# Moving one batch's tail rows to the last block of a fused linear-attention and MLP kernel

## The chip, the cores and the metric

The kernel runs on one core of one Trainium2 chip. The metric is the device time of one launch in microseconds (us). Inputs and output are float32 in device memory (HBM); all matrix products run in bf16 with float32 accumulation.

## The reference

Eight batches of eight heads, 576 positions, head size 64. Cosine-weighted linear attention is followed by a two-layer MLP with a sigmoid-approximated GELU over the 4608 rows of 512 columns:

```python
def phi(x, c, s):                       # c, s: cos and sin of pi/2 * position / 576
    r = np.maximum(x, 0.0)
    return np.concatenate([r * c, r * s], axis=-1)      # 64 -> 128 features
q_p, k_p = phi(q, cos_w, sin_w), phi(k, cos_w, sin_w)
kv  = np.einsum('bhsf,bhsd->bhfd', k_p, v)
z   = np.sum(k_p, axis=2)
x   = einsum('bhsf,bhfd->bhsd', q_p, kv) / (einsum('bhsf,bhf->bhs', q_p, z) + 1e-6)
# heads side by side: x is 4608 x 512
h   = x @ w_in                          # w_in  512 x 2048
g   = h * (1.0 / (1.0 + np.exp(-1.702 * h)))
out = g @ w_out                         # w_out 2048 x 512
```

## The kernel before, in words

**Blocks and tails.** A block is the MLP of one batch, and while TensorE runs it, the attention of the next batch is prepared. Of the 576 rows of a batch, 512 go through the block: `mm1(b, fc)` makes one of 16 slices of the hidden layer (4 matmuls of 128x512 into a PSUM tile `mm`, then ScalarE's GELU into `g`), and `mm2(b, t, lo, hi)` sums the slices `lo` to `hi` into output chunk `t` of 128 rows (one 128x512 matmul for each slice). After the last slice ScalarE copies the chunk to `ysb`, and a DMA stores it. The 64 rows left over of each batch are its tail. Tails lie side by side in `xt` (before the GELU) and `gt` (after it), 64 columns for each batch. Two neighbouring tails make one output chunk, `mm2(u, 4, ...)` for u = 1, 3, 5, 7.

**Where the tails are worked.** The tails of batches 0 and 1 are worked early by `mm1_tail_first`: 2 x 32 matmuls of 64 columns for each of these batches, at the end of that batch's first layer. Their chunk, `mm2(1, 4, 0, FC)`, stands in block 1. The other six tails are worked in the last block by `mm1_tails(fc)`: 64 matmuls of 384 columns in all.

**Preparing the next batch inside a block.** VectorE makes the weighted features of q (`trig_q`, into `qn`) and k (`trig`, into `kr`), and casts v into `vt` (`vcopy`). DMA transposes turn `qn` into `qT` (`qturn_dma`, line 196). Then TensorE makes k^T v (`kv_mm`, line 214; 72 matmuls, evacuated to `kvs` by VectorE in `kv_evac`), and for each of five chunks of 128 rows the numerators and denominators (`num_mm`, line 227; 8 matmuls). VectorE divides (`num_div`, lines 235 to 239, result `xn`), and a DMA transpose writes `xn` into the input `xT` of the next block (`xturn_dma`, line 268; chunk 4, the tail, goes to `xt`). I call these five chunks x0 to x4. The first matmul of the next block reads all 512 columns of `xT`, thus x0 to x3.

**Order.** The program text sets the order on every engine (`manual_schedule`): each engine takes its instructions as they are written, and waits only on data and buffers. In block 1 TensorE has, after its first layer: the tail of batch 1 (line 300), k^T v of batch 2, the tails' chunk (16 matmuls), and then four output chunks in halves of 8 matmuls, with x0 to x4 of batch 2 behind the first five halves. Blocks 2 to 6 do the same without the two tail steps. `pat` holds two PSUM tiles (`at`) for k^T v and the numerators, `pmm` four for all else.

**Queues.** SyncE's queue (SP) issues, in the order of the program, the transposes and, from `load_next`, the loads of q, k and v two batches ahead; POOL's queue issues the early loads and the stores of line 335. Only the very last half chunk is stored from SP.

Of the kernel before, what the change touches and what calls it, by code (L numbers as in the profile page):

```python
# [11 lines left out]
AF = mybir.ActivationFunctionType  # L12
# [7 lines left out]
def kernel(  # L20
# [9 lines left out]
    nc = tc.nc  # L30
    B, H, S, D = q.shape
    d_model = H * D
    d_ff = moe_w_in.shape[1]
    KC = d_model // 128
    FC = d_ff // 128
# [85 lines left out]
    def wcol(kc, fc):  # L121

        g, c = divmod(fc, 4)
        w = w_in_t[g][:, kc, :] if g < 2 else w_in_t[2][:, kc, ts(g - 2, 512)]
        return w.rearrange("p (f c) -> p f c", c=4)[:, :, c]
# [68 lines left out]
    def qturn_dma(c):  # L194
        n = 128 if c < 4 else 64
        nc.sync.dma_start_transpose(out=qT[:, :, c * 128:c * 128 + n],
                                    in_=qn[0:n, c].rearrange("p h f -> p (h f)"))
# [3 lines left out]
    def kv_open(i0=0, i1=NI):  # L201
        t = pat.tile([128, 2, 512], F32, name="at")
        for i in range(i0, i1):
            st["kv", i] = t[:, :, ds((i - i0) * 65, 65)]
        st["ps", i0] = t[:, :, 0:(i1 - i0) * 65]
        if i0 == 0:
            st["kvs"] = small.tile([128, 2, NI, VW], BF16, name="kvs", bufs=2)

    def kv_mm(i0, i1, rhs, col, n):
        for i in range(i0, i1):  # L210
            for j in range(NS):
                for hh in range(2):
                    r = slice(hh * 64, hh * 64 + 64)
                    nc.tensor.matmul(st["kv", i][:, hh, ds(col, n)], kr[r, j, i, :], rhs(r, i, j),  # L214
                                     start=(j == 0), stop=(j == NS - 1))

    def kv_evac(i0, i1):
        o = st["kvs"][:, :, i0:i1, 0:65]
        nc.vector.tensor_copy(o, st["ps", i0].rearrange("p hh (i e) -> p hh i e", e=65))  # L219
# [3 lines left out]
    def num_mm(c):  # L223
        ps = pat.tile([128, 2, 512], F32, name="at")
        for h in range(H):
            i, hh = divmod(h, 2)
            nc.tensor.matmul(ps[:, h // 4, ds((h % 4) * 65, 65)], qT[:, h, ts(c, 128)],  # L227
                             st["kvs"][:, hh, i, 0:65], start=True, stop=True)
        nums[c] = [ps]

    def num_div(c):
        ps = nums[c][0]
        pv = ps[:, :, 0:260].rearrange("p a (h e) -> p a h e", h=4)
        den = small.tile([128, 2, 4], F32, name="den")
        nc.vector.tensor_scalar(den, pv[:, :, :, 64], 1e-6, None, op0=ADD)  # L235
        inv = small.tile([128, 2, 4], F32, name="inv")
        nc.vector.reciprocal(inv, den)  # L237
        xn = small.tile([128, 2, 4, 64], BF16, name="xn", bufs=4)
        nc.vector.tensor_tensor(xn, pv[:, :, :, 0:64],  # L239
                                inv.unsqueeze(3).to_broadcast([128, 2, 4, 64]), op=MUL)  # L240
        nums[c].append(xn)
# [6 lines left out]
    def x_cols(b, c):  # L248
        return x[b][:, :, ts(c, 128)] if c < 4 else xt[:, :, ts(b, 64)]
# [15 lines left out]
    def xturn_dma(b, c):  # L265
        xn = nums.pop(c)[1]
        n = 128 if c < 4 else 64
        nc.sync.dma_start_transpose(out=x_cols(b, c),
                                    in_=xn[0:n].rearrange("p a h e -> p (a h e)"))
# [17 lines left out]
    def mm1(b, fc):  # L287
        mm1_part(b, fc, 0, MT)
        gelu(fc)
# [3 lines left out]
    xt = one.tile([128, KC, B * 64], BF16, name="xt")  # L293
    gt = one.tile([128, FC, B * 64], BF16, name="gt")

    def mm1_tail_first(b, half):
        hps = pmm.tile([128, 8, 64], F32, name="mm")
        for f in range(8):
            for kc in range(KC):
                nc.tensor.matmul(hps[:, f], wcol(kc, half * 8 + f), xt[:, kc, ts(b, 64)],  # L300
                                 start=(kc == 0), stop=(kc == KC - 1))
        nc.scalar.activation(gt[:, ts(half, 8), ts(b, 64)], hps, AF.Gelu_apprx_sigmoid)

    def mm1_tails(fc):
        hps = pmm.tile([128, MT], F32, name="mm")
        for kc in range(KC):
            nc.tensor.matmul(hps[:, 128:B * 64], wcol(kc, fc), xt[:, kc, 128:B * 64],  # L307
                             start=(kc == 0), stop=(kc == KC - 1))
        nc.scalar.activation(gt[:, fc, 128:B * 64], hps[:, 128:B * 64], AF.Gelu_apprx_sigmoid)

    yp = {}
    out_j = out[0:S].rearrange("(p j) d -> j p d", j=NS)
# [1 line left out]
    def rows(b, t):  # L314

        if t == 4:
            return [(64 * u, 64, out_j[NS - 1] if b + u == 1 else out[(b + u) * S - 64:(b + u) * S])
                    for u in range(2)]
        if b == 0:
            return [(64 * u, 64, out_j[2 * t + u]) for u in range(2)]  # L320
        return [(0, 128, out[b * S:b * S + 512].rearrange("(p c) d -> c p d", c=4)[t])]

    def mm2(b, t, lo, hi, c0=0, c1=d_model, last=False):
        if lo == 0:
            yp[b, t, c0] = pmm.tile([128, d_model], F32, name="mm")
        for fc in range(lo, hi):
            w = gT[fc][:, ts(t, 128)] if t < 4 else gt[:, fc, ts(b // 2, 128)]
            nc.tensor.matmul(yp[b, t, c0][:, c0:c1], w, w_out_sb[:, fc, c0:c1],  # L328
                             start=(fc == 0), stop=(fc == FC - 1))
        if hi == FC:  # L330
            ysb = ypool.tile([128, d_model], F32, name="ysb")
            nc.scalar.activation(ysb[:, c0:c1], yp[b, t, c0][:, c0:c1], AF.Identity)  # L332
            for p0, n, dst in rows(b, t):
                eng = nc.sync if last else nc.gpsimd
                eng.dma_start(out=dst[:, c0:c1], in_=ysb[p0:p0 + n, c0:c1])  # L335

    def idle(n, cols=512):
# [10 lines left out]
    def start_block(b, opened=False):  # L348

        if not opened:  # L350
            xturn_mm(0)
            xturn_evac(b, 0)
            xturn_mm(1)
            xturn_evac(b, 1)
            num_mm(2)
            num_div(2)
        for c in range(4):
            for fc in range(4):
                mm1_part(b, fc, c * 128, c * 128 + 128)
            if c == 0:  # L360
                num_mm(3)
                num_div(3)
                xturn_mm(2)
                xturn_evac(b, 2)
            if c == 1:
                num_mm(4)
                num_div(4)
                xturn_mm(3)
                xturn_evac(b, 3)
        for fc in range(4):  # L370
            gelu(fc)
        mm1(b, 4)
        xturn_mm(4)
        xturn_evac(b, 4)
# [52 lines left out]
        trig(kr, kf, j)  # L427
    for fc in range(5, FC):
        mm1(0, fc)
    mm1_tail_first(0, 0)  # L430
    mm1_tail_first(0, 1)
    for c in range(5):
        trig_q(c, act=(c > 2))
        qturn_dma(c)
# [27 lines left out]
    mm2(0, 3, 12, 16)  # L462
    start_block(1, opened=True)


    for b in range(1, B):
        nb = b + 1 if b + 1 < B else None
        f0 = 5 if b == 1 else 0
        for fc in range(f0, FC):
            if nb is not None and fc == f0:  # L470
                for c in range(5):
                    trig_q(c)
                    qturn_dma(c)
            if nb is not None and fc == f0 + 1:
                for j in range(NS):
                    trig(kr, kf, j)
                vcopy(0, 4)
                if nb + 1 < B:
                    load_next(nb + 1)
            mm1(b, fc)  # L480
        if nb is not None:
            x_open(nb)
        if b == 1:
            mm1_tail_first(1, 0)
            mm1_tail_first(1, 1)
        if nb is not None:
            kv_open()
            kv_mm(0, 4, vt_rhs, 0, 65)
            kv_evac(0, 4)
        if b == 1:  # L490
            mm2(1, 4, 0, FC)
        if nb is None:
            for fc in range(FC):
                mm1_tails(fc)
            for u in range(3, B, 2):
                mm2(u, 4, 0, FC)
        for t in range(4):
            last = nb is None and t == 3
            if last:
                mm2(b, t, 0, FC, 0, 256)  # L500
                mm2(b, t, 0, FC, 256, 512, last=True)
                continue
            mm2(b, t, 0, 8)
            if nb is not None and t < 3:
                num_mm(2 * t)
                num_div(2 * t)
                xturn_dma(nb, 2 * t)
            mm2(b, t, 8, 16)
            if nb is not None and t < 2:
                num_mm(2 * t + 1)  # L510
                num_div(2 * t + 1)
                xturn_dma(nb, 2 * t + 1)


# [28 lines left out]
```

## Time and profile before

| What | Value |
|---|---|
| Median of 3 runs (lowest, highest) | 294.02 us (294.0, 294.31) |
| The profiled execution: its own time | 294.29 us |
| Its span, first to last instruction | 292.6 us |
| TensorE busy | 284.0 us, 97% of the span |
| VectorE, ScalarE, POOL busy | 123.6, 128.7, 57.5 us |
| Mean granted TensorE clock | 0.998 |
| DMA traffic | 53.54 MB; q1 (issued by SP) 35.53 MB, q0 (by POOL) 17.63 MB |

The profile is of one execution, whose own time lies 0.27 us above the median. Times in it count from its first instruction. PE is TensorE's matrix unit, DVE is VectorE, ACT is ScalarE; SPq and POOLq are the instruction sequencers of SyncE and GpSimd. The chain of waits is the work that ended last, followed backwards from the end, and shows in what order the time was spent.

### The profile page before, as it was taken

To read this page: it belongs to the slowest core of one execution; us is meant where nothing else is said; L and a number is where in the kernel's file an instruction comes from. 1 tells how busy PE (TensorE), PEld (TensorE's weight loads), DVE (VectorE), ACT (ScalarE), POOL (GpSimd) and SP (SyncE) were. 2 spreads that over 40 slices of the span, in tenths; PEclk is the share of its full clock that TensorE was granted. 3 is DMA by queue.
4 is the path that set the end of the run, shared out by engine and by line. 5 is a ranking of instruction groups with operands and counts; after the bars stand their busy time and mean duration, and the time that the engine had idled before them with its cause. 6 is when DMAs were issued, how large, how long until landed. Compare 5 with 4: busy or idle time off the path is not lost.

```text
span 292.6 us, 6031 instructions
## 1 busy us (share of the span) xinstructions
PE 284.0 (97%) x2461; PEld 157.6 (54%) x2461; DVE 123.6 (42%) x355; ACT 128.7 (44%) x224; POOL 57.5 (20%) x70
## 2 busy tenths in 40 slices
PE   8979999999999999999999999999999999999993
PEld 3775646857545554555555554555455545564452
DVE  4774415881478047903691269225931510000000
ACT  7947733663116611562146304631464136771111
POOL 6350003200216001600061014201330110001211
PEclk9999999999999999999999999999999999999999
DMA  7999999999989964999598859895840430001311
GB/s 252 240 224 286 347 179 238 370 205 245 382 161 182 303 248 116 176 249 312 136 176 243 306 142 166 208 357 137 152 99 2 104 97 25 1 0 38 72 72 72
DMA packets 72731, 53.54 MB, mean 183 GB/s; under 512 B 52608, under 2 KB 62464, under 8 KB 72704
## 3 DMA queue, kind: packets, MB, share of 16 engines
q1 hardware_dynamic: 66160, 35.53, 49.6%
q0 software_dynamic: 6544, 17.63, 22.5%
q8 instruction: 19, 0.31, 0.4%
q14 instruction: 8, 0.07, 0.1%
HBM read 36.70 MB, written 9.44 MB: 158 GB/s over the span
## 4 chain that ended last, share of the span: by engine, by line
PE 93%; DMA 4%; DVE 1%; POOL 0%; issue 0%; ACT 0%; ACTq 0%
PE mm L328 43%; PE mm L279 38%; PE mm L307 4%; PE at L227 3%; PE at L214 3%; DMA vb<-in_v_dram 2%; PE mm L300 1%; DMA kf<-in_k_dram 1%; PE at L256 1%; DVE xn L239 1%; POOL vb L139 0%; DVE inv L237 0%; PE mm L182 0%; DVE den L235 0%; ACT ysb L332 0%
## 5 line engine op out<-in xcount | busy, mean ns | idle before, releaser
L328 PE MATMUL mm<-w_out_sb,g 128*128 128x512 bf16 (+1 forms) x528 | 117.4, 372 | 0.0
L279 PE MATMUL mm<-xT,w_in 128*128 128x512 bf16 (+1 forms) x608 | 113.5, 345 | 0.0
L284 ACT ACTIVATE g<-mm 128x512 bf16<-128x512 f32 x128 | 75.6, 598 | 32.0 <-PE mm L279 31.9
L335 POOL DMA_DIRECT2D out_dram<-ysb x44 | 46.4, 1057 | 216.8 <-ACT ysb L332 216.7
L279 PEld LDWEIGHTS <-w_in 128*128 128x128 bf16 x608 | 61.7, 113 | 49.1
L328 PEld LDWEIGHTS <-g 128*128 128x128 bf16 x528 | 48.8, 98 | 50.0
L332 ACT ACTIVATE ysb<-mm 128x512 f32<-128x512 f32 (+1 forms) x37 | 21.7, 586 | 115.8 <-PE mm L328 115.8
L219 DVE CAST kvs<-at 128x520 bf16<-128x520 f32 (+1 forms) x9 | 5.8, 642 | 56.4 <-PE at L214 56.4
L239 DVE TENSOR_TENSOR xn<-at,inv 128x512 bf16<-128x512 f32 x40 | 27.6, 691 | 1.4
L153 DVE TENSOR_SCALAR kr<-kf,cosw 128x256 bf16<-128x256 f32 x68 | 23.3, 343 | 9.1 <-DMA kf<-in_k_dram 9.1
L153 DVE TENSOR_SCALAR kr<-kf,sinw 128x256 bf16<-128x256 f32 x68 | 23.5, 346 | 0.0
L235 DVE TENSOR_SCALAR den<-at 128x8 f32<-128x8 f32 x40 | 6.6, 166 | 37.1 <-PE at L227 37.1
L227 PEld LDWEIGHTS <-qT 128*128 128x128 bf16 x320 | 14.5, 97 | 7.3
L166 DVE TENSOR_SCALAR qn<-qf,cosw 128x512 bf16<-128x512 f32 (+1 forms) x33 | 15.7, 477 | 3.8 <-DMA qf<-in_q_dram 3.8
L227 PE MATMUL at<-kvs,qT 128*128 128x65 bf16 x320 | 15.9, 193 | 0.0
L166 DVE TENSOR_SCALAR qn<-qf,sinw 128x512 bf16<-128x512 f32 (+1 forms) x33 | 15.8, 477 | 0.0
L328 PE MATMUL mm<-w_out_sb,gt 128*128 128x512 bf16 x64 | 14.2, 379 | 0.0
L214 PEld LDWEIGHTS <-kr 64*128 64x128 bf16 x648 | 10.3, 94 | 4.0 <-issue 3.1
L307 PE MATMUL mm<-xt,w_in 128*128 128x384 bf16 x64 | 10.6, 326 | 0.0
L328 PEld LDWEIGHTS <-gt 128*128 128x128 bf16 x64 | 6.2, 97 | 7.3
L174 DVE CAST vt<-vf 128x2304 bf16<-128x2304 f32 (+1 forms) x7 | 8.9, 1264 | 0.6 <-DMA vf<-in_v_dram 0.6
L307 PEld LDWEIGHTS <-w_in 128*128 128x128 bf16 x64 | 7.2, 113 | 3.3
(57 smaller groups left out, 101.5 us busy)
## 6 DMA issues: line engine op xcount, KB each, us to landing
kf<-in_k_dram SPq DMA_DIRECT2D x6, 1152.0 KB, 9.4
vf<-in_v_dram SPq DMA_DIRECT2D x6, 1152.0 KB, 12.3
out_dram<-ysb POOLq DMA_DIRECT2D x27, 256.0 KB, 2.7
qf<-in_q_dram SPq DMA_DIRECT2D x6, 1024.0 KB, 6.9
out_dram<-ysb POOLq DMA_DIRECT2D x17, 128.0 KB, 6.1
w_out_sb<-in_moe_w_out_dram POOLq DMA_DIRECT2D x4, 512.0 KB, 18.1
kf<-in_k_dram POOLq DMA_DIRECT2D x1, 1152.0 KB, 12.3
vf<-in_v_dram POOLq DMA_DIRECT2D x1, 1152.0 KB, 20.6
```

The costliest lines, as they stand in the source:

```text
L153: nc.vector.tensor_scalar(o, i, 0.0, w[:, j:j + 1], op0=MAX, op1=MUL)
L166: nc.vector.tensor_scalar(o, i, 0.0, sc, op0=MAX, op1=MUL)
L174: nc.vector.tensor_copy(o, i)
L214: nc.tensor.matmul(st["kv", i][:, hh, ds(col, n)], kr[r, j, i, :], rhs(r, i, j), start=(j == 0), stop=(j == NS - 1))
L227: nc.tensor.matmul(ps[:, h // 4, ds((h % 4) * 65, 65)], qT[:, h, ts(c, 128)], st["kvs"][:, hh, i, 0:65], start=True, stop=True)
L239: nc.vector.tensor_tensor(xn, pv[:, :, :, 0:64], inv.unsqueeze(3).to_broadcast([128, 2, 4, 64]), op=MUL)
L279: nc.tensor.matmul(hp[fc][:, t0:t1], wcol(kc, fc), x[b][:, kc, t0:t1], start=(kc == 0), stop=(kc == KC - 1))
L284: nc.scalar.activation(g, hp.pop(fc), AF.Gelu_apprx_sigmoid)
L307: nc.tensor.matmul(hps[:, 128:B * 64], wcol(kc, fc), xt[:, kc, 128:B * 64], start=(kc == 0), stop=(kc == KC - 1))
L328: nc.tensor.matmul(yp[b, t, c0][:, c0:c1], w, w_out_sb[:, fc, c0:c1], start=(fc == 0), stop=(fc == FC - 1))
L332: nc.scalar.activation(ysb[:, c0:c1], yp[b, t, c0][:, c0:c1], AF.Identity)
L335: eng.dma_start(out=dst[:, c0:c1], in_=ysb[p0:p0 + n, c0:c1])
```

## The change

Three things change. `mm1_tail_first` is called for batch 0 alone, and `mm1_tails` covers 448 columns in place of 384; the chunk of the tails of batches 0 and 1, `mm2(1, 4, ...)`, moves from block 1 to the last block. In block 1 k^T v of batch 2 comes after the whole first output chunk (`kv_next`), x0 and x1 come together after the first half of the second chunk, and x2, x3, x4 after one further half each; blocks 2 to 6 keep their order. In the last block every store is issued by SP and none by POOL.

```diff
-    def mm1_tail_first(b, half):
+    def mm1_tail_first(half):
         hps = pmm.tile([128, 8, 64], F32, name="mm")
         for f in range(8):
             for kc in range(KC):
-                nc.tensor.matmul(hps[:, f], wcol(kc, half * 8 + f), xt[:, kc, ts(b, 64)],
+                nc.tensor.matmul(hps[:, f], wcol(kc, half * 8 + f), xt[:, kc, 0:64],
                                  start=(kc == 0), stop=(kc == KC - 1))
...
     def mm1_tails(fc):
         hps = pmm.tile([128, MT], F32, name="mm")
         for kc in range(KC):
-            nc.tensor.matmul(hps[:, 128:B * 64], wcol(kc, fc), xt[:, kc, 128:B * 64],
+            nc.tensor.matmul(hps[:, 64:B * 64], wcol(kc, fc), xt[:, kc, 64:B * 64],
                              start=(kc == 0), stop=(kc == KC - 1))
-        nc.scalar.activation(gt[:, fc, 128:B * 64], hps[:, 128:B * 64], AF.Gelu_apprx_sigmoid)
+        nc.scalar.activation(gt[:, fc, 64:B * 64], hps[:, 64:B * 64], AF.Gelu_apprx_sigmoid)
...
-    def mm2(b, t, lo, hi, c0=0, c1=d_model, last=False):
+    def mm2(b, t, lo, hi, c0=0, c1=d_model, end=False):
...
-                eng = nc.sync if last else nc.gpsimd
+                eng = nc.sync if end else nc.gpsimd
...
+    def kv_next():
+        kv_open()
+        kv_mm(0, 4, vt_rhs, 0, 65)
+        kv_evac(0, 4)
+
+    def x_next(b, c):
+        num_mm(c)
+        num_div(c)
+        xturn_dma(b, c)
...
-        if b == 1:
-            mm1_tail_first(1, 0)
-            mm1_tail_first(1, 1)
-        if nb is not None:
-            kv_open()
-            kv_mm(0, 4, vt_rhs, 0, 65)
-            kv_evac(0, 4)
-        if b == 1:
-            mm2(1, 4, 0, FC)
+        if nb is not None and b > 1:
+            kv_next()
         if nb is None:
             for fc in range(FC):
                 mm1_tails(fc)
-            for u in range(3, B, 2):
-                mm2(u, 4, 0, FC)
+            for u in range(1, B, 2):
+                mm2(u, 4, 0, FC, end=True)
         for t in range(4):
...
+            if nb is None:
+                for c in range(2 if t == 3 else 1):
+                    n = 256 if t == 3 else 512
+                    mm2(b, t, 0, FC, c * n, c * n + n, end=True)
                 continue
...
+            for u in range(2):
+                mm2(b, t, 8 * u, 8 * u + 8)
+                s = 2 * t + u
+                if b > 1:
+                    if s < 5:
+                        x_next(nb, s)
+                elif s == 1:
+                    kv_next()
+                elif 1 < s < 6:
+                    for c in (0, 1) if s == 2 else (s - 1,):
+                        x_next(nb, c)
```

More of the change, by code (lines that the diff above doesn't have):

```diff
@@ L299, in mm1_tail_first @@
             for kc in range(KC):
-                nc.tensor.matmul(hps[:, f], wcol(kc, half * 8 + f), xt[:, kc, ts(b, 64)],
+                nc.tensor.matmul(hps[:, f], wcol(kc, half * 8 + f), xt[:, kc, 0:64],
                                  start=(kc == 0), stop=(kc == KC - 1))
-        nc.scalar.activation(gt[:, ts(half, 8), ts(b, 64)], hps, AF.Gelu_apprx_sigmoid)
+        nc.scalar.activation(gt[:, ts(half, 8), 0:64], hps, AF.Gelu_apprx_sigmoid)
     def mm1_tails(fc):
@@ L429 @@
         mm1(0, fc)
-    mm1_tail_first(0, 0)
-    mm1_tail_first(0, 1)
+    mm1_tail_first(0)
+    mm1_tail_first(1)
     for c in range(5):
@@ L494 @@
                 mm1_tails(fc)
-            for u in range(3, B, 2):
-                mm2(u, 4, 0, FC)
+            for u in range(1, B, 2):
+                mm2(u, 4, 0, FC, end=True)
         for t in range(4):
[L498 to L501, printed above, removed]
+            if nb is None:
+                for c in range(2 if t == 3 else 1):
+                    n = 256 if t == 3 else 512
+                    mm2(b, t, 0, FC, c * n, c * n + n, end=True)
                 continue
[L503 to L512, printed above, removed]
+            for u in range(2):
[9 more added lines that the diff above has]
+                        x_next(nb, c)
 _INS = ['q', 'k', 'v', 'moe_w_in', 'moe_w_out']
```

## The prediction

> **What bounds the kernel now.** I read the page first, then the chain of waits, then SP's timeline with the landing times in block 1, then the end. The page's first and fourth parts:
>
> ```profile
> PE 284.0 (97%) x2461; PEld 157.6 (54%) x2461; DVE 123.6 (42%) x355; ACT 128.7 (44%) x224; POOL 57.5 (20%) x70
> ...
> PE 93%; DMA 4%; DVE 1%; POOL 0%; issue 0%; ACT 0%; ACTq 0%
> ```
>
> TensorE is the bound: from 23 us to 287.5 us the chain leaves it for 0.02 us at most at a time. An edit therefore counts if it changes TensorE's work, makes TensorE wait, or changes what follows its last matmul. The chain through block 1 (start, us, what):
>
> ```profile
> 66.50 2.13 PE mm L300 x64
> 68.62 1.19 PE at L214 x72
> 69.81 5.29 PE mm L328 x24
> 75.10 0.24 PE at L227 x8
> 75.34 1.73 PE mm L328 x8
> ...
> 81.01 0.24 PE at L227 x8
> 81.25 1.73 PE mm L328 x8
> 82.98 0.24 PE at L227 x8
> 83.22 5.18 PE mm L328 x24
> 88.40 3.67 PE mm L279 x17
> ```
>
> Line 300 is the tail of batch 1, line 214 k^T v, the 24 matmuls of 5.29 us the tails' chunk (16) and half an output chunk. The four L227 pieces are the numerators; x3's end at 81.25, and block 2 starts at 88.40 without a wait. The same stretch on SP, and then the landing of x3's transpose alone:
>
> ```profile
> 68.40 0.63 SPq L114 DMA_DIRECT2D qf<-in_q_dram  x1
> 69.12 0.57 SPq L109 DMA_DIRECT2D kf<-in_k_dram  x1
> 69.79 0.44 SPq L109 DMA_DIRECT2D vf<-in_v_dram  x1
> 76.54 7.12 SPq L268 DMA_TRANSPOSE xT<-xn  x4
> ```
>
> ```profile
> L268 SPq DMA_TRANSPOSE xT<-xn x1: 1216/1216/1216, 82.4 to 82.4; - x1
> DMA to landing us min/median/max: 3.9/3.9/3.9
> ```
>
> The loads for batch 3 stand on the queue ahead of the transposes. That of v, issued at 69.8, takes 11.9 us and lands at 81.7. x0, issued at 76.5, lands after it, at 82.1 (5.6 us, where the quickest transpose of the run takes 2.3 and the median 2.6); x1 at 83.4, x2 at 85.4, x3 at 86.4. So here the queue serves in order, and x0 waits for v. x3 is 2.0 us ahead of its use. The end, by line 538 (count: duration ns min/median/max, first and last start):
>
> ```profile
> L538 POOLq DRAIN x3: 51/102/5292, 286.5 to 292.3; - x3
> L538 SPq DRAIN x3: 7/7/13, 290.1 to 292.1; - x3
> ```
>
> POOL's last store is issued at 286.52; its closing drain runs 5.29 us from 286.50 to 291.79. SP's last store lands at 289.9, SP's drain begins at 290.1, and the rest is ready too. Hence the final exchange of semaphores, which runs from 291.84 to 292.55, waits 1.7 us for POOL alone.
>
> **The tail of batch 1.** Block 1 loses 64 matmuls of 64 columns: 2.13 us. The last block's 64 matmuls of line 307 take 10.40 us at 384 columns, 0.423 ns a column; 64 more columns in each are 64 x 64 x 0.423 = 1.73 us. Net -0.40 us. Its bound from the rows: a matmul of 448 columns lies between that of 384 (0.1625 us) and of 512 (0.2157), so the addition lies between 0 and 3.4 us, and the row at 512 gives 0.421 ns a column too; I keep 1.73. Two GELUs go; sixteen grow from 384 to 448 columns, 0.49 to some 0.54 us, under 0.76 us of matmul each, so they stay hidden. Without that cover each would cost 0.05 us.
>
> **The tails' chunk.** 16 matmuls, 3.45 us, leave block 1 and come back in the last block: 0. Its two stores (issued 74.35 and 74.87) leave POOL and the DMA engines in block 1. In the last block its last matmul needs the sixteenth GELU, 0.5 us of work behind 15 matmuls (3.2 us).
>
> **k^T v and the x steps.** The matmuls are the same; the 0.10 us that the first eight after k^T v cost more (1.83 against 1.73) stays once. TensorE's new order from 66.50, if it never waits: first chunk to 69.95, k^T v to 71.14, eight matmuls to 72.97, x0 and x1 to 73.45, eight to 75.18, x2 to 75.42, eight to 77.15, x3 to 77.39, eight to 79.12, x4 to 79.36, the last chunk to 82.81. Block 2 could start at 82.8, 5.6 us earlier than before. k^T v's inputs are ready (the v cast ends at 66.18). Its evacuation (0.70 us, done by 71.9) hides behind the eight matmuls that follow; without them it would cost about 0.8. The third `at` tile is that of x0, free after its division at 74.4, needed at 75.18. x0's and x1's divisions follow each other on VectorE, 1.04 us apart in the rows at 14.20 and 15.24.
>
> From the end of the numerators to the issue of the transpose takes 1.2 us (81.25 to 82.44). So x0 is issued at 74.4, x1 at 75.6 (SP holds each for 1.22), x2 at 76.8, x3 at 78.6. Landing in the undisturbed 2.6 us, x3 would be there at 81.2, 1.6 ahead of block 2: no wait. But they queue behind v, whose load was issued at 69.8 and isn't moved. x0 then lands at 82.2 as before, and x1, x2, x3 follow one by one.
>
> How fast? Low end: from 82.0 to 83.3 the DMA engines served 1086 packets of q1, and one lone transpose is 546 (107.7 to 109.0), so two pass in 1.3 us, 0.6 to 0.65 each; x3 lands at 84.0. High end: the gaps of before, 1.3, 1.9 and 1.0 us, x3 at 86.4. I take 0.85 each, x3 at 84.7, nearer to the low end: x3 itself, issued only at 82.4, could not have landed before 84.8, and x2's gap holds a 16 KB instruction fetch and a store. The wait of TensorE is then 84.7 - 82.8 = 1.9 us, between 1.2 and 3.6; nothing if v lands two microseconds sooner. v may move by 0.6 us either way, since other stores now share the engines with it. The wait isn't made up later: TensorE is the bound, and VectorE and SP prepare batch 3 some 3 us sooner too, so x3's lead in block 2 (issued 112.6, landing 115.2, used at 118.5) stays near 3 us.
>
> **Stores from SP.** Thirteen stores are issued by SP in the last block, twelve of them moved there, 0.36 to 0.63 us of SP each, two at most per 1.7 us, with nothing queued behind them but later stores. SP's last store stays as it is. POOL then ends with block 6's last store, issued at 240.1 before and some 3.7 us earlier now, so a drain of 5.3 us is over by 243. The final exchange starts when SP is done at 290.14, not at 291.84: -1.65 us, leaving 0.05 for the hand-over. At worst, 0.
>
> A rule speaks against this: the Trainium skill, "DMA: Bandwidth & Descriptors", section "Issuing engines are not separate DMA queues", says that issuing from another engine only saves the sequencer's issue time. By it this part would be worth nothing, as these issues are hidden. The row of the 5.29 us drain says otherwise for the end; I follow the row.
>
> **Sum.** From the profiled execution: 294.29 - 0.40 - 1.65 + 1.9 = 294.14. That execution is 0.27 above the median of 294.02, and the span lies 1.7 under it on both sides of the change; from the median, 293.9. What a measurement of this kernel can tell from no change is about 0.2%, 0.59 us.
>
> **Rivals.**
> 1. *Little or no wait.* x3 lands before 83.9. For it: lone transposes take 2.3 to 2.6 us, all four would be issued by 78.6, and one busy engine held up x0 (from 80.6 to 81.2 only 7 packets of q1 moved). Against: the landings follow the order of issue, and v landed at 81.7. The sum is -2.05 plus a wait of 0 to 1.1: 292.0 to 293.1.
> 2. *Slower: the queue sets block 2's start.* The transposes keep the old gaps or a store falls between them, x3 lands between 85.1 and 86.4 or a little later, the wait is 2.3 to 3.6 us or more: 294.3 to 295.6. It decides against the change from x3 at 84.9, where the wait is 2.05. For it: the four gaps measured. Against: x3's own late issue then.
> 3. *The stores from SP bring nothing*, because the drain or another closing step takes as long elsewhere: 294.02 - 0.40 + 1.9 = 295.5. The rule just cited would give this. For it: nothing in the trace shows POOL draining early. Against: SP, which issues transposes and loads all along, drains in 0.01 us.
>
> A wait above 3.4 us would by the Trainium skill, "TensorE: Matmul & The Clock Gate", section "What's actually happening", halve the clock for some microseconds. No gap of TensorE over 0.8 us is in this trace after the start, so no row shows it.
>
> **How the numbers follow.** Forecast (x3 lands at 83.9 to 85.1 and the end moves; 293.1 to 294.3): 0.42. Rival 1: 0.25. Rival 2: 0.21. Rival 3: 0.12. The wait below which the time falls by over 0.59 is 2.05 - 0.59 = 1.46; 0.12 of the forecast lies there. So faster 0.25 + 0.12 = 0.37. Within: 0.30 of the forecast and 0.02 of rival 2, 0.32. Slower: 0.19 and 0.12, 0.31. As both signs are open, the likeliest case's own range is 293.1 to 294.3; the whole range runs from no wait, 292.0, to rival 2's and 3's 295.5.
>
> **What would show it.** Right: no L300 in block 1, L307 near 12.1 us; block 2 starts after an idle of TensorE that x3's transpose ends; v lands near 81.7 and x0 right behind it; POOL's long drain starts near 237, and the span ends 0.8 us after SP's drain begins. Wrong: no idle ahead of block 2 (rival 1), one over 2.6 us (rival 2), POOL or another engine later than SP at the end (rival 3), or any wait at k^T v or at a numerator.

## The result and the profile after

The changed kernel takes 297.89 us in the median of 21 runs (294.17 to 299.78), the kernel before 294.21 us in the median of 21 (293.9 to 295.53): 3.7 us slower. The ratio of the two is given as 1.0061 with a 95% interval of 1.0039 to 1.0083, some 1.8 us; it rests on the runs within 1.5% of each kernel's fastest and leaves out the nine slowest of the changed kernel (298.7 to 299.8), none of which was traced. By either number the change is slower. The profiled execution took 297.89 us, its span is 296.2 us.

The profile's groups first (busy us, mean ns, then idle time before and what ended it), the first layer before the change and then two groups after it:

```profile
L279 PE MATMUL mm<-xT,w_in 128*128 128x512 bf16 (+1 forms) x608 | 113.5, 345 | 0.0
```

```profile
L279 PE MATMUL mm<-xT,w_in 128*128 128x512 bf16 (+1 forms) x598 | 114.4, 349 | 3.9 <-DMA xT<-xn 3.4
...
L307 PE MATMUL mm<-xt,w_in 128*128 128x448 bf16 x64 | 12.3, 353 | 0.0
```

The first layer now waits 3.4 us for a transpose; before it waited for nothing. The chain of waits shows where (start, us, what):

```profile
66.08 3.61 PE mm L328 x16
69.70 1.19 PE at L214 x72
...
76.90 0.24 PE at L227 x8
...
81.10 4.80 DMA xT<-xn
85.91 0.09 issue
86.00 5.74 PE mm L279 x18
91.73 0.05 issue
91.78 9.88 PE mm L279 x45
101.66 1.19 PE at L214 x72
```

The order is the new one: the first chunk (16 matmuls), k^T v, the numerators, with x3's ending at 77.1. Then the chain leaves TensorE for x3's transpose, issued at 81.10 and landing at 85.9. A second loss stands behind it: 18 matmuls take 5.74 us, 319 ns each, where 45 further ones take 220. Block 2's first layer thus lasts 15.66 us (86.00 to 101.66). Before, it was one piece of the chain:

```profile
88.40 13.81 PE mm L279 x64
```

The timeline of the same stretch gives the two waits (idle us and what ended it, in brackets) and SP's side:

```profile
69.52 1.16 SPq L109 DMA_DIRECT2D vf<-in_v_dram  x1
74.16 8.37 SPq L268 DMA_TRANSPOSE xT<-xn  x4
83.94 0.69 DVE L239 TENSOR_TENSOR xn<-at,inv 128x512 bf16<-128x512 f32 x1 [4.39 <-DMA xT<-xn]
86.00 6.17 PE L279 MATMUL mm<-xT,w_in 128*128 128x512 bf16 x19 [3.43 <-DMA xT<-xn]
```

v is issued at 69.5 and lands 12.8 us later, at 82.3. x0 is issued at 74.2 and lands 9.7 us later, at 83.9. x1's issue alone takes 3.72 us, so that x3's cannot start before 81.1; why SP is held there no run shows. VectorE also waits, for x0's transpose to free one of the four `xn` buffers, but only for x4. The stages around the wait (stretch, us, busy of PE, PEld, DVE, ACT, POOL, then granted clock, DMA share, GB/s; packets overlap, so a DMA share can pass 1):

```profile
82.30:86.00 3.70, 0.27 (x3) 0.03 (x1) 2.06 (x5) 0.60 (x1) 0.54 (x1) 1.00 1.17 268
86.00:88.00 2.00, 2.00 (x6) 0.78 (x7) 2.00 (x6) 0.59 (x1) 0.00 (x0) 0.63 0.61 112
88.00:90.00 2.00, 2.00 (x6) 0.73 (x5) 2.00 (x8) 0.61 (x2) 0.00 (x0) 0.51 0.98 182
90.00:92.00 2.00, 1.95 (x9) 1.01 (x9) 2.00 (x9) 1.19 (x2) 0.00 (x0) 1.00 1.05 199
```

The second loss is the clock: 0.63 and 0.51 of full speed in the two stretches from 86 to 90. It is at half from 86.5 to 90.0, so it fell half a microsecond after TensorE was back. The end, by line 543 (the same closing code as line 538 before):

```profile
L543 POOLq DRAIN x3: 51/93/4435, 239.5 to 295.9; - x3
L543 SPq DRAIN x3: 7/13/130, 294.9 to 295.7; - x3
```

POOL's long drain now starts at 239.5, far from the end. From the end of ScalarE's last copy to the end of the span it is 3.6 us (292.6 to 296.2), against 4.6 before (288.0 to 292.6).

### The profile page after: what moved, and what is told of

Same layout as the page of the kernel before. It is cut to its first block, busy times and chain, and to the rows that moved or that the text cites. A ratio compares the mean times of both kernels' runs of the same rounds, so it can differ in the third digit from the quotient of the medians.

```text
span 296.2 us, 5879 instructions
## 1 busy us (share of the span) xinstructions
PE 283.4 (96%) x2363; PEld 155.5 (53%) x2397; DVE 123.7 (42%) x355; ACT 128.2 (43%) x222; POOL 46.4 (16%) x58
## 4 chain that ended last, share of the span: by engine, by line
PE 90%; DMA 3%; ACT 2%; DVE 1%; issue 1%; SPq 1%; ACTq 0%
PE mm L328 41%; PE mm L279 36%; PE mm L307 4%; PE at L214 3%; PE at L227 3%; DMA kf<-in_k_dram 2%; DMA xT<-xn 2%; ACT g L284 1%; ACT kr L151 1%; PE at L256 1%; PE mm L300 1%; PE mm L182 1%; DVE xn L239 1%; SPq L268 0%; DVE inv L237 0%
## 5 line engine op out<-in xcount | busy, mean ns | idle before, releaser
L328 PE MATMUL mm<-w_out_sb,g 128*128 128x512 bf16 (+1 forms) x507 | 115.7, 373 | 1.4 <-issue 0.3
L335 POOL DMA_DIRECT2D out_dram<-ysb x32 | 35.4, 1109 | 180.8 <-ACT ysb L332 180.7
L153 DVE TENSOR_SCALAR kr<-kf,cosw 128x256 bf16<-128x256 f32 x68 | 23.9, 352 | 9.4 <-DMA kf<-in_k_dram 9.4
L307 PE MATMUL mm<-xt,w_in 128*128 128x448 bf16 x64 | 12.3, 353 | 0.0
L309 ACT ACTIVATE gt<-mm 128x448 bf16<-128x448 f32 x16 | 8.7, 543 | 3.3 <-PE mm L307 3.2
```

The lines of the kernel that those rows point to most:

```text
L153: nc.vector.tensor_scalar(o, i, 0.0, w[:, j:j + 1], op0=MAX, op1=MUL)
L307: nc.tensor.matmul(hps[:, 64:B * 64], wcol(kc, fc), xt[:, kc, 64:B * 64], start=(kc == 0), stop=(kc == KC - 1))
L309: nc.scalar.activation(gt[:, fc, 64:B * 64], hps[:, 64:B * 64], AF.Gelu_apprx_sigmoid)
```

## The experiments

**The end alone.** The kernel before, with the stores of the last block on SP:

```diff
             for u in range(3, B, 2):
-                mm2(u, 4, 0, FC)
+                mm2(u, 4, 0, FC, last=True)
...
-                mm2(b, t, 0, FC, 0, 256)
+                mm2(b, t, 0, FC, 0, 256, last=True)
...
-            mm2(b, t, 8, 16)
+            mm2(b, t, 8, 16, last=(nb is None))
```

> The kernel before with the last block's stores on SP, the tails left where they were. The end theory (POOL's closing drain of 5.3 us, started by its last store, holds the final exchange): TensorE's chain does not change, the final exchange starts when SP is done; in the changed kernel that was 3.3 us after TensorE's last matmul against 4.3 before, so -1.0 us, 293.0 us, and its runs agree within 0.3 us. The rival (issuing from another engine brings nothing at the end): 294.0 us. Neither expects a wait ahead of block 2.

Measured: 292.11 us (291.93 to 292.49), ratio 0.9933 (0.9921 to 0.9945). By line 538:

```profile
L538 POOLq DRAIN x3: 51/93/4543, 239.9 to 290.3; - x3
L538 SPq DRAIN x3: 7/7/13, 289.8 to 290.1; - x3
```

POOL's drain starts at 239.9, and the span ends 2.8 us after ScalarE's last copy. The rival, that nothing is won at the end, is out. The gain of 1.9 us is larger than the 1.0 expected: the changed kernel loses a part of it again (below).

**How long the drain holds.** The kernel before, with only the first half of the last chunk moved to SP:

```diff
-                mm2(b, t, 0, FC, 0, 256)
+                mm2(b, t, 0, FC, 0, 256, last=True)
```

> The kernel before with one store more on SP: the first half of the last chunk, so that POOL's last store is issued near 285.0 and not 286.5. The drain theory (4.7 us from the end of POOL's last store issue): POOL's drain ends near 290.2, about when SP is done, and the end comes 1.4 to 1.5 us sooner: 292.6 us. If a drain of POOL in the last block costs the same whenever it starts, 294.0 us.

Measured: 292.38 us, ratio 0.9925 (0.9897 to 0.9952).

```profile
L538 POOLq DRAIN x3: 51/93/5209, 284.6 to 290.3; - x3
L538 SPq DRAIN x3: 7/7/13, 289.6 to 290.1; - x3
```

The drain takes 5.2 us again, from 284.6 to 289.8, and ends about when SP is done. It starts with POOL's last store, which is now the one before, issued 1.9 us sooner (284.6 for 286.5). That alone brings nearly all of the gain.

**v's load behind x3.** The changed kernel, with one load moved on SP's queue:

```diff
     def load_next(b):
 
         load_q(b, nc.sync)
         load(kf, k, b, nc.sync)
-        load(vf, v, b, nc.sync)
+        if b != 3:
+            load(vf, v, b, nc.sync)
...
                         x_next(nb, c)
+                    if s == 4:
+                        load(vf, v, 3, nc.sync)
```

> The changed kernel, with the load of v for batch 3 alone moved on SP's queue from ahead of the four transposes x0 to x3 to behind x3. The queue theory (x0 to x3 wait behind v in SP's queue): they then follow k, which lands near 79; x3 is issued near 78.3 and lands by 81.5, TensorE waits at most 0.3 us ahead of block 2 and the clock stays full: 294.0 - 0.4 - 1.0 = 292.6 us. The order theory (x1 to x3 are late because their numerators come later in block 1): the wait of 3.6 us and the slow clock stay, 297.9 us. The contention theory (stores and loads share the engines, the order on the queue does not matter): v's bytes only move to the same stretch, the wait shrinks by no more than 1 us, 296 us or more.

Measured: 292.2 us (292.01 to 292.89), ratio 0.9938 (0.9925 to 0.9951). The chain from the last numerators into block 2, and the landing of x3 (issued at 79.0):

```profile
79.18 0.24 PE at L228 x8
79.42 3.45 PE mm L329 x16
82.87 3.88 PE mm L280 x18
```

```profile
L269 SPq DMA_TRANSPOSE xT<-xn x1: 1219/1219/1219, 79.0 to 79.0; - x1
DMA to landing us min/median/max: 3.5/3.5/3.5
```

x3 lands at 82.5 and TensorE goes on without a wait; block 2's first layer takes 13.8 us. With one load out of the transposes' way the wait is gone, and the clock loss with it. By itself this run doesn't tell the order on the queue from a mere sharing of the DMA engines, since v's bytes now move behind x3. The changed kernel's packets do, in the stretch from 74.5 to 79.0 us:

```profile
DMA packets 769, 1.83 MB, mean 406 GB/s; under 512 B 32, under 2 KB 32, under 8 KB 768
```

x0 had been issued at 74.2 and x1 at 75.5, and a lone transpose is 546 packets, all but one under 512 B (107.7 to 109.0 us in the trace before). Only 32 so small moved, so the transposes stood still while the loads ahead of them ran.

**k^T v first.** The changed kernel, with block 1 in the order of the other blocks:

```diff
-        if nb is not None and b > 1:
+        if nb is not None:
             kv_next()
...
-                if b > 1:
-                    if s < 5:
-                        x_next(nb, s)
-                elif s == 1:
-                    kv_next()
-                elif 1 < s < 6:
-                    for c in (0, 1) if s == 2 else (s - 1,):
-                        x_next(nb, c)
+                if s < 5:
+                    x_next(nb, s)
```

> The changed kernel with block 1 in the order of blocks 2 to 6: k^T v ahead of the first output chunk, x0 to x4 behind the first five halves, so that x3's numerators end near 75.2 and not 77.1. TensorE's work is the same. The queue theory: x0 to x3 still stand behind v, which lands near 82; x3 lands no more than 1 us sooner, the wait stays above 2 us: 295 to 298 us. The order theory: x3 lands 2 us sooner, the wait falls to 1.6 us and the clock stays full: 294.2 us.

Measured: 297.37 us (295.64 to 299.26), ratio 1.0117 (1.0087 to 1.0148). x0's transpose, issued 3.5 us sooner than in the changed kernel:

```profile
L268 SPq DMA_TRANSPOSE xT<-xn x1: 2206/2206/2206, 70.6 to 70.6; - x1
DMA to landing us min/median/max: 12.0/12.0/12.0
```

It lands at 82.6 all the same, behind v (81.6); x3 lands at 85.6, TensorE waits 3.2 us, and the clock falls to 0.50. The new order of block 1 is not the cause.

**Without block 1's stores.** The changed kernel, without the stores of block 1's first three output chunks:

```diff
-            for p0, n, dst in rows(b, t):
+            for p0, n, dst in rows(b, t)[(b == 1 and t < 3):]:
```

> The changed kernel without the stores of block 1's first three output chunks (384 rows of batch 1 are not written). The turns theory (the two 256 KB stores that POOL issues between 75 and 80 us take turns of about 0.75 us on the DMA engines between x0 to x3): v lands up to 0.7 us sooner and x3 lands 1.5 to 2 us sooner, near 84, the wait falls from 3.6 to about 2 us and the clock stays full: 293.9 to 295 us. The rival (the transposes behind the loads are slow by themselves): x3 lands near 85.5 as before, 297 us or more.

Measured: 293.3 us (292.4 to 294.43), ratio 0.9958 (0.9935 to 0.9981). v, issued at 68.4, lands after 11.0 us at 79.5; x3, issued at 78.7, lands after 2.8 us at 81.5, and in the trace TensorE doesn't wait. The effect is larger than expected: v comes 2.8 us sooner and x3 4.4. Of v's 2.8 us, 1.1 stem from its issue, which was that much sooner before any of these stores would have been issued (70.7); the stores cost it the other 1.7. x0 lands 0.5 us behind v, where it was 1.6 in the changed kernel. The median lies 0.6 us above the traced execution; what the others lose was not traced. In the changed kernel the DMA packets show how stores and transposes pass, from 83.5 to 84.2 and from 84.25 to 85.0 (queue, packets, MB, share of 16 engines):

```profile
q0 software_dynamic: 57, 0.23, 83.2%
q1 hardware_dynamic: 60, 0.01, 8.8%
...
q1 hardware_dynamic: 766, 0.19, 128.5%
q0 software_dynamic: 13, 0.00, 1.2%
```

A store is 64 packets of 4 KB. While one moves, the transposes nearly stand still, and then the other way round. So the wait has two parents: v ahead in SP's queue, and POOL's stores, which hold up v and then fall between the transposes.

**The stores behind x3.** The changed kernel with all its output; block 1's first two chunks are stored from SP after x3's transpose:

```diff
+            if b == 1 and t < 2:
+                late.append((ysb, t))
+                return
             for p0, n, dst in rows(b, t):
...
                         x_next(nb, c)
+                    if s == 4:
+                        for ysb, tt in late:
+                            nc.sync.dma_start(out=rows(1, tt)[0][2], in_=ysb)
```

> The changed kernel with all its work, where block 1's first two output chunks are stored from SP behind x3's transpose and not from POOL as soon as they are copied. The turns theory (these two stores hold up v and the transposes): v lands near 79.5, x3 near 81.5 as without the stores, no wait ahead of block 2: 292.4 us in the median, less 0.1 to 0.2 if the wait for the last store stands later in SP's closing order (15 stores from SP). The rival (the kernel without stores was fast because bytes were missing, not because of when they move): the wait stays near 2 us, 295 us.

Measured: 294.17 us (292.4 to 295.31), ratio 0.9983 (0.9963 to 1.0002). The traced execution, 293.02 us, has v at 80.6, x3 at 82.6 and no wait. But the median lies above it, so it was traced again:

> The kernel with block 1's first two stores behind x3 on SP, traced a second time. Its first trace had no wait ahead of block 2 at 293.0 us, its median is 294.2. If the wait comes back in some executions, a time near 294.2 shows an idle time of 1 to 1.5 us ahead of block 2 that x3's transpose ends; if not, the trace shows where else TensorE waits.

The second execution took 294.23 us. TensorE's line at the start of block 2 in its timeline:

```profile
84.16 3.19 PE L279 MATMUL mm<-xT,w_in 128*128 128x512 bf16 x14 [1.65 <-ACT ysb L333]
```

The line names ScalarE as what came last, but that copy was done at 83.2; x3 landed at 84.07 (issued at 79.0, 5.0 us), right after the third chunk's store from POOL (83.84). In the first execution that store was issued 0.6 us later (80.4 for 79.8) and landed 1.1 us behind x3. The wait is back at 1.65 us, and 294.23 less that is 292.6. Two stores out of the way are not always enough.

**The clock.** The changed kernel with 16, and then with 8, matmuls on constant data ahead of block 2:

```diff
                         x_next(nb, c)
+        if b == 1:
+            idle(16)
```

> The changed kernel with 16 matmuls on constant data (3.45 us at the full rate, results unused) between block 1's last output chunk and block 2. The clock theory (a wait of 3.6 us lets the granted clock fall to about half for some 4 us): the clock stays at 1.0, block 2's first layer takes 13.8 us and not 15.7, block 2 still starts when x3 has landed near 86: 297.9 - 1.85 = 296.0 us in the profiled run, and the runs spread by less than 2 us against 5.6. The rival (block 2's first matmuls are slow because transposes, loads and VectorE work beside them): they stay slow, 297.9 us.

Measured: 297.09 us (296.1 to 297.6), ratio 1.0097 (1.0076 to 1.0118). The stages of the traced execution (columns as above): the filled stretch, the wait that is left, and block 2:

```profile
82.40:85.85 3.45, 3.45 (x16) 1.37 (x14) 2.04 (x5) 0.60 (x1) 0.54 (x1) 1.00 1.21 254
85.85:86.44 0.59, 0.00 (x0) 0.03 (x1) 0.59 (x3) 0.00 (x0) 0.00 (x0) 1.00 1.00 291
86.44:88.44 2.00, 1.95 (x9) 1.07 (x11) 2.00 (x7) 0.67 (x2) 0.00 (x0) 1.00 0.82 147
```

The clock stays at 1.00 and the first layer takes 13.98 us (86.44 to 100.42), although VectorE, the transposes and the loads work beside it as before. So the slow matmuls are the clock and nothing else, but for 0.17 us. The six runs spread by 1.5 us, where the 21 of the changed kernel spread by 5.6. The traced execution, 296.66 us, is 0.7 us above the expectation, of which x3's landing at 86.4 explains 0.4. Two of the six have a mean clock of 0.991 and 0.992; they were not traced.

> The changed kernel with 8 matmuls on constant data (1.73 us) before block 2, where the kernel with 16 had 3.45. Block 2 still starts when x3 lands, near 86, so TensorE sits idle for about 2 us and not 3.6. If the clock falls only after an idle time near 3.4 us, it stays at 1.0 and the runs lie at 296 to 297.5 us as with 16 matmuls. If any idle time of some microseconds lowers it, the mean clock falls to about 0.995 and the runs spread up to 299 us.

Measured: 296.45 us (295.5 to 298.83), ratio 1.0079 (1.0049 to 1.0109). The traced execution sat idle for 1.69 us and kept its clock. Nine of the twelve runs lie at 295.5 to 296.8 with a mean clock of 0.997 or more, three at 298.3 to 298.8 with 0.991 or 0.992; those were not traced, so whether a longer wait or something else lowered their clock stays open.

**The changed kernel, traced three times more.** No edit.

> The changed kernel, traced a second time. The theory (its time is 292.6 us plus the wait ahead of block 2 plus what the fallen clock costs behind it): the time is that sum within 0.4 us in each traced execution, whatever the wait, and the clock falls only where the wait is above about 3 us. The rival (something else in the kernel varies from run to run): the sum misses by more than 1 us.

> The changed kernel, traced a third time; expected as for the second.

> The changed kernel, traced a fourth time; expected as for the second.

| Execution | Time | Idle ahead of block 2 | Its first layer, over 13.81 | What is left |
|---|---|---|---|---|
| profiled first | 297.89 | 3.43 | 1.85 | 292.6 |
| third | 298.14 | 3.73 | 1.85 | 292.6 |
| fourth | 297.68 | 3.14 | 1.66 | 292.9 |
| second | 295.10 | 0.62 | 0.17 | 294.3 |

Three of four have a wait of 3.1 to 3.7 us and a fallen clock; less these two the rest is 292.6 to 292.9. The fourth trace's stages show the clock falling already before TensorE starts again at 85.88 (0.89 over two microseconds is 0.4 us at half):

```profile
84.00:86.00 2.00, 0.12 (x1) 0.15 (x2) 2.00 (x6) 0.00 (x0) 0.25 (x1) 0.89 1.09 293
86.00:88.00 2.00, 2.00 (x6) 0.64 (x5) 2.00 (x6) 0.21 (x1) 0.00 (x0) 0.50 0.70 130
88.00:90.00 2.00, 2.00 (x9) 0.91 (x8) 2.00 (x9) 0.98 (x2) 0.00 (x0) 0.76 0.96 185
```

In the second the wait is short, as TensorE itself comes to block 2 only at 84.2 and not at 82.6, and the clock stays; yet its sum misses by 1.6 us. The cause lies at the start, where the expectation had left room for a rival:

```profile
10.00:15.00 5.00, 4.95 (x102) 3.95 (x101) 2.48 (x8) 3.89 (x8) 2.78 (x6) 0.66 1.23 206
```

From 10 to 15 us its clock is 0.66, and block 1's first layer ends 1.6 us later than in the first trace (67.68 against 66.08). That stretch is the same code in both kernels. Hence the traced runs spread for three reasons: the wait, the clock behind it, and sometimes the clock at the start. What the nine slowest executions lose beyond the 298.1 us of the third trace stays open.

**Where the end loses 0.4 us.** The kernel with v behind x3, and the two stores of the first tails' chunk back on POOL:

```diff
             for u in range(1, B, 2):
-                mm2(u, 4, 0, FC, end=True)
+                mm2(u, 4, 0, FC, end=(u > 1))
```

> The kernel with the v load behind x3, with the two stores of the chunk of the tails of batches 0 and 1 back on POOL in the last block, so that SP issues 11 stores there and not 13. The closing-order theory (SP ends with nine waits in a fixed order of semaphores, and with 13 stores the last store's stands third, so that six more waits of 0.06 us come after it): the last store's wait comes last again as in the kernel with the end alone, the time from ScalarE's last copy to the end falls from 3.1 to 2.7 us: 291.8 us; POOL's drain, started near 269, is over by 275. The rival (that the 0.4 us lay elsewhere): 292.2 us.

Measured: 292.43 us (291.65 to 293.82), ratio 0.9933 (0.9904 to 0.9961). The traced execution took 291.65; from ScalarE's last copy to the end it is 2.8 us, with v behind x3 alone it was 3.2. So that part is as expected, but the median was not: 0.6 us above the forecast, with runs spread over 2.2 us. It was run again beside the kernel with the end alone:

> The kernel before with the stores of the last block on SP, again, beside the next one on one chip: 292.1 us.

> The changed kernel with v's load behind x3 and the tails' chunk stored by POOL, again. The sum of the parts (TensorE 0.40 us less, no wait, the same end as in the kernel with the end alone): 0.4 us under that kernel on the same chip, 291.7 us. The rival (a wait of some runs eats it): within 0.1 us of it or above, and the runs spread over more than 1 us.

Measured: 292.28 us (292.08 to 293.67), ratio 0.993 (0.9907 to 0.9954), for the end alone; 291.77 us (291.66 to 293.19), ratio 0.9914 (0.9891 to 0.9937), with the tails joined and v behind x3. The difference of the medians is 0.5 us where the sum of the parts gives 0.4. This is the quickest median seen, 2.5 us under the 294.3 us of the kernel before on that chip. But the two intervals overlap, and the same kernel's first ratio, 0.9933, is that of the end alone. So it isn't shown that the joined tails gain anything beyond what the end alone gains.

## Why the prediction was wrong

- **Sign and size.** 293.9 us with 292.0 to 295.5 was forecast, 297.89 measured, outside the range. Rival 2, the queue that sets block 2's start, happened. Its wait of 2.3 to 3.6 us or more was met with 3.43; the fallen clock, which it didn't price, came on top.
- **TensorE's work: right.** Line 300's 2.13 us left block 1, and line 307's 64 matmuls take 12.11 us on the chain against 10.40: -0.42, forecast -0.40. The tails' chunk cost nothing, no wait stands at k^T v or at the numerators.
- **The order on the queue: right.** x0 landed behind v in every trace in which v stands ahead of it and its landing is known, and the wait went with v's load.
- **v "may move by 0.6 us either way": too little.** It landed 0.6 us later by the clock of the trace in an execution that ran 0.4 us ahead. From issue to landing it took 12.8 to 12.9 us in three traces, where the four with the old block 1 have 11.4 to 12.0, so the change makes it 0.8 to 1.5 us longer. Without block 1's stores it took 11.0, and the times of issue of these stores are what the change moves (70.7 and 75.9, against 74.4 to 74.9 and 78.1).
- **"x0 then lands at 82.2 as before", and so x3 at 84.7: the step that failed.** x3 landed at 85.8 to 86.1 in three of four traces, and the wait was 3.1 to 3.7 us and not 1.9. The 0.85 us for each further transpose was not what was wrong: from x0 to x3 it was 2.1 to 2.4 us, where the prediction has 2.5. x0 itself landed at 83.4 to 83.9, because v came at 82.3 to 82.4 and x0 1.0 to 1.6 us behind it. The prediction took the 0.5 us between them from a single trace; the four traces whose block 1 is that of the kernel before range from 0.4 to 1.6 (1.5 and 0.4 with the end alone, 1.6 with only half the last chunk moved). Where stores were out of the way it was 0.5 each time.
- **SP's issues, "1.22" each: wrong for x1.** Its issue held SP for 3.7 us, so x3 was issued 2.5 us late, at 81.1. That alone doesn't explain the landing at 85.9, as 2.6 us behind 81.1 is 83.7. The rows of x0 to x3 in the kernel before (1.2 us each) didn't show that SP can be held, but others of the same trace did, such as a transpose of `qn` in block 1:

```profile
L196 SPq DMA_TRANSPOSE qT<-qn x1: 3071/3071/3071, 59.9 to 59.9; - x1
```

- **The clock: left out of the sum.** The prediction kept it as a sentence on waits above 3.4 us, without a chance. It cost some 1.5 to 1.7 us in the three long waits: the first layer took 1.66 to 1.85 us longer, and 0.17 of this stands in three traces with a full clock too. The Trainium skill, "TensorE: Matmul & The Clock Gate", section "What's actually happening", has the half clock after an idle window of about 3.4 us. The traces agree on the half (0.50), but less idle time was enough: in the fourth trace TensorE had stood still for 2.8 us when the clock fell (85.5 us), and with k^T v first for 2.6 (85.1 us). After waits of 1.69 us and less it stayed full.
- **The end: right in kind, off in size.** By itself it is worth 1.9 us, 1.65 forecast. In the changed kernel it is only 1.0: 0.4 us goes since with 13 stores the last store's semaphore is waited for third of nine, and another 0.4 us lies between SP's two closing drains (294.90 and 295.29, where 0.06 us separates them in the kernel with v behind x3). What causes that second part was not settled. The Trainium skill's rule in "DMA: Bandwidth & Descriptors", section "Issuing engines are not separate DMA queues", that another issuing engine saves only the issue time, doesn't hold for the end of this program (1.9 us).
- **Block 2 and later: right.** x3 of batch 3 landed at 114.65, 3.3 us ahead of block 3.

The sum with the measured terms, from the profiled 294.29: -0.42 for TensorE, -1.0 for the end, +3.43 for the wait, +1.85 for the slower first layer, -0.4 for the earlier start of this execution, is 297.75, against 297.89.

## What to carry to other kernels

Work that is taken out ahead of a stage also takes away the time in which that stage's inputs arrive: look at what stands ahead of them on their queue and what else uses the DMA engines then, and price the wait by the landings measured under that load. A wait of TensorE that may reach some 3 us is to be priced with the clock behind it. A value taken from one trace, such as the 0.5 us between two landings, is to be given a range. Stores issued by POOL should end some 5 us before the program does, by the drains seen here.

## What the runs showed of the hardware

- POOL's closing drain took 5.2 to 5.3 us behind a store issued in the last microseconds, and 4.4 to 4.6 us behind one after which all else ran on for 25 to 50 us more.
- A DMA transpose behind a load and between stores took up to 12.0 us to land, against 2.3 to 2.6 alone, and its issue could hold SP for 5.5 us (x1 with k^T v first), against 1.2.
- The granted clock fell to half in or behind waits of 3.1 to 3.7 us and stayed there for 3.4 us each time: from 86.5, 87.5 and 85.5 us in three traces, where TensorE was back at 86.0, 86.2 and 85.9. A wait of 1.7 us left it at 1.00.
